# Converting 64-bit weights without a maximum and a mask, and a new order of the first query loads, in an attention and gated-layer kernel

## The chip, the cores and the metric

One Trainium2 chip, one core of it. The metric is the time of one execution on the device in microseconds (us); three runs of the kernel before give a median of 1798.62 us (1796.67 to 1802.75).

TensorE (PE in the rows) multiplies matrices, with its weight loads (PEld) beside it; VectorE is DVE, ScalarE is ACT, GpSimd is POOL, and SP is the engine that issues most transfers. TensorE writes to PSUM banks, the others read them from there; everything else lies in SBUF tiles.

## What is computed

Attention on keys and values pooled by 8, then a gated layer, then a layer with a rational activation, all in float32 accuracy:

```python
k_p = k.reshape(B, H, Sp, 8, D).mean(axis=3)      # B = H = 8, S = 576, D = 64
v_p = v.reshape(B, H, Sp, 8, D).mean(axis=3)
attn = softmax(q @ k_p.T / sqrt(D));  x = attn @ v_p        # 4608 tokens, 512 columns
g = x @ w_gate                                    # 512 x 1536
x = (g * sigmoid(g) * (x @ w_val)) @ w_out        # 1536 x 512
h = x @ w_in                                      # 512 x 2048
out = (P(h) / (Q(h) + 1e-6)) @ w_out2             # 2048 x 512
```

All weights come as 64-bit floating-point numbers, two 32-bit words each, and are converted on the chip.

## The kernel before

**Blocks.** The 4608 tokens are worked in 9 blocks of 512. Blocks 0 to 2 go one by one through the gated layer (`PLAIN = 3`, stages j = 0, 1, 2), the other six in pairs with a Strassen-like scheme whose sums of weights are made in stages 1 and 2 and streamed from DRAM. The last layer runs over all 9 blocks at the end.

**One step.** Each stage loops over f = 0 to 11, one 128-column part of the 1536. A step has 12 matmuls for the gate (`gp`), 12 for the value (`vp`) and 12 for the output (`acc`, of the step before). Each product is three: high by high, low by high, high by low part (`mm3`, line 256), so a weight is needed in two tiles, `w[:, 0]` (the high part, written by ScalarE, line 165) and `w[:, 1]` (the low part, a subtraction on VectorE, line 149). The first four matmuls of a product use the high parts alone; the next four need the low part of the weight. In stage 0 the step also converts the three weights of a later step (`first.step(6)` at three places of the step). VectorE has besides the gate's product `hh` (line 803) and the low part `ht` (line 808).

**Conversion of a weight** (`conversion`, from line 102). A raw tile holds the two words of each number. ScalarE takes the absolute value of the high word, read as float32 (L110), and scales the low word (L111). VectorE takes a maximum (L120), shifts left by 3 and masks (L121), and joins the sign (L114, `select`). GpSimd adds the low word (L117). The result goes to ScalarE for the high part and to VectorE for the low part. The tiles are called `tg`, `tv`, `to` and `rawg`, `rawv`, `rawo` for gate, value and output weights of the gated layer (36 conversions, 128 x 512, class `Weights`), and `rawi`, `rawo` for the last layer (64 conversions of 128 x 256, class `Halves`, in the later stages). In `Weights.step` the ScalarE part of one weight, the VectorE and GpSimd part of the one begun before, the rounding of the one before that and the last subtraction of a fourth stand one behind another.

**Attention.** A unit is up to 128 tokens of one batch entry. For block 0 there are four (0, 128, 256, 384), worked before the gated layer starts: scores (line 368, 32 products for two units), maximum and difference or scaled maximum (lines 376 to 385), exponential on ScalarE (389, 394), sum and reciprocal (401 to 403), normalisation on GpSimd (404), copies (412), transposes on TensorE (429, 433), their evacuation (436, 437, 441), and the products with the values (457, 460). The values are summed on VectorE (305) and masked on GpSimd (318 to 334). For block 1 the units 0 to 4 run inside stage 0, from f = 5 on, at fixed places of the step: scores behind one step, the maximum, the exponential and the sum in the next, the transposes (line 429) ahead of the value product of the one after.

**Order.** There is no scheduler: each engine's instructions run in the order in which the code writes them, and each queue issues its loads in order. A tile's buffer comes free when its last reader is done; a load into it waits for that in SP's queue.

Of the kernel before, what the change touches and what calls it, by code (L numbers as in the profile page):

```python
# [10 lines left out]
F32 = mybir.dt.float32  # L11
F32R = mybir.dt.float32r
U32 = mybir.dt.uint32
AF = mybir.ActivationFunctionType
ALU = mybir.AluOpType
# [48 lines left out]
def attention_gated_rational(  # L64
# [4 lines left out]
    nc = tc.nc  # L69
# [11 lines left out]
    def f32(ap):  # L81
        return ap.bitcast(F32)
# [14 lines left out]

    LEAST = float(np.uint32(0x38000000).view(np.float32))  # L100

    def conversion(key, raw, n, spare, t=None):

        hi_word, lo_word = raw[:, :, 1], raw[:, :, 0]
        if t is None:
            t = ldp.tile([P, 512], F32, tag="ld", name=f"t{key}")[:, :n]
        tu = t.bitcast(U32)

        def words():
            nc.scalar.activation(t, hi_word.bitcast(F32), AF.Abs)  # L110
            nc.scalar.activation(lo_word, lo_word, AF.Copy, scale=2.0 ** -29)  # L111

        def select():
            nc.vector.scalar_tensor_tensor(  # L114
                hi_word, hi_word, 0xC0000000, tu, op0=ALU.bitwise_and, op1=ALU.bitwise_or
            )
            nc.gpsimd.tensor_tensor(tu if spare else hi_word, hi_word, lo_word, op=ALU.add)  # L117

        bits = [
            lambda: nc.vector.tensor_scalar(t, t, LEAST, None, op0=ALU.max),  # L120
            lambda: nc.vector.tensor_scalar(  # L121
                tu, tu, 3, 0x3FFFFFFF, op0=ALU.logical_shift_left, op1=ALU.bitwise_and
            ),
            select,
        ]
        return words, bits, t if spare else f32(hi_word)

    class Weights:
# [14 lines left out]
        def step(self, ahead, eng=None):  # L143
            begun = None
            middle, rounded, last = self.stages
            if last:
                key, spare, _, t = last
                w = self.done[key]
                (eng or nc.vector).tensor_tensor(w[:, 1, :], t, f32(w[:, 0, :]), op=ALU.subtract)  # L149
                live["w"] -= not spare  # L150
            if self.raws:
                key, raw, spare = self.raws.pop(0)
                words, bits, t = conversion(key, raw, 512, spare)
                words()
                begun = key, spare, bits, t
            if middle:
                for fn in middle[2]:
                    fn()
                live["w"] -= middle[1]
            if rounded:  # L160
                live["w"] += 1
                assert live["w"] <= WSLOTS
                key, t = rounded[0], rounded[3]
                w = self.done[key] = wslot(f"w{key}")
                nc.scalar.activation(w[:, 0, :], t, AF.Copy)
            self.stages = [begun, middle, rounded]
            while self.next < len(self.items) and len(self.raws) < ahead:
                if live["w"] + (self.next < self.spare or any(x and not x[1] for x in self.stages)) >= WSLOTS:
                    break
                self.load()  # L170
# [5 lines left out]
    class Halves:  # L176
# [26 lines left out]
        def begin(self, n=1, more=1):  # L203
            self.store()
            for _ in range(more):
                self.load()
            self.now = []
            for key, h, tile_, raw in [self.raw.pop(0) for _ in range(min(n, len(self.raw)))]:
                t = f32(tile_[:, 512:768])
                words, bits, _ = conversion(f"{key}_{h}", raw, 256, True, t)  # L210
                words()
                self.now.append((key, h, tile_, t, bits))
# [57 lines left out]
    def at_load(src, name, early, n=512, eng=None, parts=P):  # L270
        t = wslot(name, (P, 512), F32) if early else ldp.tile([P, 512], F32, tag="ld", name=name)
        (eng or nc.sync).dma_start(t[:parts, :n], src)
        return t
# [201 lines left out]
    def qload(u, early=False, eng=None):  # L475
        b, s, n, o = u
        off = NPAIR * (b * S + s)
        return at_load(q[:, off : off + NPAIR * n], f"q{b}_{s}", early, NPAIR * n, eng)
# [50 lines left out]
    flat0 = [u for g in g0 for u in g]  # L529
    qts = {flat0[0]: qload(flat0[0], True, nc.scalar)}  # L530
    qts[flat0[1]] = qload(flat0[1], True)
    nc.scalar.dma_start(ident, ident_in)
    nc.scalar.dma_start(vmask, vmask_in)
    nc.scalar.activation(vr[:, :, 0, :], ident[:, :D].unsqueeze(1).to_broadcast([P, NPAIR, D]), AF.Copy, scale=0.0)
    vruns = [jb() for jb in jobs[5:]]
    for u in flat0[2:]:
        qts[u] = qload(u, True)
    nc.scalar.dma_start(cab[:, 0:4], ca)
    nc.scalar.dma_start(cab[:, 4:6], cb)

# [12 lines left out]
        r()  # L553
    x = [keep.tile([P, 2, BLK], F32R, tag=f"x{kk}", name=f"x0_{kk}") for kk in range(KT)]
    soft = [scores(u, qts[u], True, heads=n < 2) for n, u in enumerate(flat0)]
    for n in range(2):
        soft[n][0]()
        soft[n][1]()
    for r in vruns:
        r()  # L560
    build_vs(0)
# [7 lines left out]
        evacs[n] = transposes(flat0[n], ptTs[n], 0, 1 + n % 2)  # L569

    last = len(flat0)
    soft[0][2]()
    soft[0][3]()
    soft[2][0]()
    soft[2][1]()
    first.step(6)
    soft[1][2]()
    soft[1][3]()
# [437 lines left out]
    def hidden_part(p, key, k):  # L1016
        while order_h and len(ahead) < 3:
            nxt = order_h[0]
            if nxt[0] != p and nxt[2] == 0 and k < NK - 1:
                break  # L1020
            ahead.append(hidden_sum(*order_h.pop(0)))
        t = ring_tile(f"h{p}{key}_{k}")
        split(t[:, 0, :], t[:, 1, :], ahead.pop(0))
        return t
# [3 lines left out]
    for p, (j1, j2) in enumerate(PAIRS):  # L1028
# [36 lines left out]
        for i, (ow, key) in enumerate(zip(O_ORDER, TOKENS)):  # L1065
# [5 lines left out]
            for k in range(NK):  # L1071
                t = hidden_part(p, key, k)
# [29 lines left out]
    with tc.tile_pool(name="p2", bufs=1, reuse_waits="tile") as p2:  # L1102
# [31 lines left out]
        for n, (j, f) in enumerate(its):  # L1134
# [11 lines left out]
            t = p2.tile([P, BLK], F32, tag="t", name=f"t{n}")  # L1146
# [93 lines left out]
```

## Time and profile before

| | us |
|---|---|
| median of three runs | 1798.62 (1796.67 to 1802.75) |
| the profiled execution | 1798.48 |
| its span, first to last instruction | 1796.7 |
| TensorE busy | 1743.1 (97%) |
| VectorE busy | 1404.0 (78%) |
| ScalarE busy | 1135.4 (63%) |
| GpSimd busy | 345.4 (19%) |

The shares are means over stages with different limits. Of the page's 40 slices of 44.9 us, TensorE is busy 6, 8, 9 and 8 tenths in the first four, and 9 in all others but the last. The mean granted clock of TensorE is 0.996. So the page sends a reader to the first 180 us, and to the rows of that stretch.

### The profile page before, as it was taken

To read this page: it belongs to the slowest core of one execution; us is meant where nothing else is said; L and a number is where in the kernel's file an instruction comes from. 1 tells how busy PE (TensorE), PEld (TensorE's weight loads), DVE (VectorE), ACT (ScalarE), POOL (GpSimd) and SP (SyncE) were. 2 spreads that over 40 slices of the span, in tenths; PEclk is the share of its full clock that TensorE was granted. 3 is DMA by queue.
4 is the path that set the end of the run, shared out by engine and by line. 5 is a ranking of instruction groups with operands and counts; after the bars stand their busy time and mean duration, and the time that the engine had idled before them with its cause. 6 is when DMAs were issued, how large, how long until landed. Compare 5 with 4: busy or idle time off the path is not lost.

```text
span 1796.7 us, 23824 instructions
## 1 busy us (share of the span) xinstructions
PE 1743.1 (97%) x8212; PEld 1423.5 (79%) x8212; DVE 1404.0 (78%) x2333; ACT 1135.4 (63%) x1994; POOL 345.4 (19%) x492
## 2 busy tenths in 40 slices
PE   6898999999999999999999999999999999999998
PEld 5677877787887887887888788888888888888887
DVE  7997665548777676546777898989898989898987
ACT  5676455546665766435455676777677777767775
POOL 3344555542454344210000000000000000000000
PEclk9999999999999999999999999999999999999999
DMA  7631756559999898999826601010101010101000
GB/s 256 215 109 59 226 184 238 198 178 330 336 371 353 278 367 297 329 365 372 317 109 234 246 1 47 1 47 1 47 1 47 1 47 1 47 1 47 1 24 24
DMA packets 157464, 285.27 MB, mean 159 GB/s; under 512 B 12320, under 2 KB 78496, under 8 KB 156320
## 3 DMA queue, kind: packets, MB, share of 16 engines
q1 hardware_dynamic: 156624, 283.43, 44.8%
q8 instruction: 65, 1.06, 0.2%
q10 hardware_dynamic: 720, 0.33, 0.1%
q14 instruction: 55, 0.45, 0.1%
HBM read 194.58 MB, written 89.13 MB: 158 GB/s over the span
## 4 chain that ended last, share of the span: by engine, by line
PE 81%; DVE 5%; ACT 3%; issue 2%; POOL 1%; DMA 1%; POOLq 0%; DVEq 0%; ACTq 0%; SPq 0%
PE acco L256 22%; PE h L256 21%; PE ca L256 9%; PE ya L1083 5%; PE cc L256 5%; PE acc L256 3%; PE vp L256 3%; PE yc L1083 3%; PE gp L256 2%; PE cb L256 2%; PE pv L457 1%; PE yb L1083 1%; PE sc L368 1%; PE t L429 1%; DMA sw<-wd 0%
## 5 line engine op out<-in xcount | busy, mean ns | idle before, releaser
L256 PE MATMUL acco<-wo,gt 128*128 128x512 f32 x1728 | 417.3, 390 | 2.8 <-ACT gt L1170 2.4
L256 PE MATMUL h<-z,wi 128*128 128x512 f32 x1728 | 414.7, 389 | 0.0
L256 PEld LDWEIGHTS acco<-wo,gt 128*128 128x128 f32 x1728 | 325.3, 188 | 71.8 <-ACT gt L1170 3.2
L256 PEld LDWEIGHTS h<-z,wi 128*128 128x128 f32 x1728 | 324.4, 188 | 67.4
L1149 ACT ACTIVATE sq<-h 128x512 f32<-128x512 f32 x144 | 86.1, 598 | 197.3 <-PE h L256 197.3
L1156 DVE SCALAR_TENSOR_TENSOR w<-sq,neg,w 128x512 f32<-128x512 f32 x144 | 108.0, 750 | 48.2 <-ACT w L1150 48.2
L256 PE MATMUL vp<-x,wv 128*128 128x512 f32 x432 | 109.5, 401 | 6.2 <-DVE wv L149 6.2
L1166 DVE SCALAR_TENSOR_TENSOR g<-t,neg,e 128x512 f32<-128x512 f32 x144 | 108.3, 752 | 5.1
L1153 ACT ACTIVATE t<-h,neg 128x512 f32<-128x512 f32 x144 | 112.0, 778 | 0.0
L1162 DVE SCALAR_TENSOR_TENSOR t<-t,neg,h 128x512 f32<-128x512 f32 x144 | 107.7, 748 | 5.1
L256 PE MATMUL gp<-x,wg 128*128 128x512 f32 x432 | 108.0, 397 | 3.1 <-DVE wg L149 3.0
L1163 DVE SCALAR_TENSOR_TENSOR e<-w,ln 128x512 f32<-128x512 f32 x144 | 98.6, 685 | 13.5 <-ACT ln L1160 13.4
L1160 ACT ACTIVATE ln<-ln,lnb 128x512 f32<-128x512 f32 x144 | 104.3, 724 | 4.7
L256 PE MATMUL acc<-ht,wo 128*128 128x512 f32 x432 | 104.7, 391 | 0.0
L1170 ACT ACTIVATE gt<-g 128x512 fp32r<-128x512 f32 x144 | 90.8, 631 | 21.8 <-DVE g L1166 21.8
L1164 DVE SCALAR_TENSOR_TENSOR e<-e,ln 128x512 f32<-128x512 f32 x144 | 99.7, 692 | 5.0
L1150 ACT ACTIVATE w<-h,cab 128x512 f32<-128x512 f32 x144 | 98.3, 683 | 3.6 <-DVE e L1163 3.6
L256 PEld LDWEIGHTS vp<-x,wv 128*128 128x128 f32 x432 | 80.5, 191 | 25.3 <-DVE wv L149 8.7
L1171 DVE TENSOR_TENSOR gt<-g,gt 128x512 fp32r<-128x512 f32 x144 | 98.9, 687 | 1.9 <-ACT gt L1170 0.8
L1161 DVE TENSOR_TENSOR t<-t,h 128x512 f32<-128x512 f32 x144 | 98.2, 682 | 0.0
L256 PEld LDWEIGHTS gp<-x,wg 128*128 128x128 f32 x432 | 79.2, 188 | 22.8 <-DVE wg L149 5.1
L256 PEld LDWEIGHTS acc<-ht,wo 128*128 128x128 f32 x432 | 80.2, 188 | 16.7
(247 smaller groups left out, 3161.2 us busy)
## 6 DMA issues: line engine op xcount, KB each, us to landing
sw<-sd SPq DMA_DIRECT2D x72, 512.0 KB, 7.7
sw<-wd SPq DMA_DIRECT2D x36, 512.0 KB, 6.2
h<-hq SPq DMA_DIRECT2D x36, 512.0 KB, 7.8
sd<-sp SPq DMA_DIRECT2D x24, 512.0 KB, 4.3
sw<-vd SPq DMA_DIRECT2D x36, 256.0 KB, 7.8
hl<-h SPq DMA_DIRECT2D x18, 512.0 KB, 6.7
hr<-h SPq DMA_DIRECT2D x18, 512.0 KB, 9.7
out<-ob SPq DMA_DIRECT2D x36, 256.0 KB, 2.2
```

The lines of the kernel that those rows point to most:

```text
L256: nc.tensor.matmul(acc, st[:, lw, cols], mv[:, rw, mcols], start=first and i == 0, stop=last and i == n - 1, skip_group_check=seeded,)
L1083: nc.tensor.matmul(banks[q], w[:, lw, cols], t[:, rw, :], start=opened and k == 0 and m == 0, stop=k == NK - 1 and m == 2, skip_group_chec ...
L1150: nc.scalar.activation(w0, hps, AF.Abs, scale=cab[:, 4:5])
L1153: nc.scalar.activation(t, hps, AF.Identity, scale=neg[:, 3:4], bias=neg[:, 2:3])
L1156: nc.vector.scalar_tensor_tensor(w0, sq, neg[:, 5:6], w0, op0=ALU.mult, op1=ALU.add)
L1160: nc.scalar.activation(ln, ln, AF.Exp, scale=-1.0, bias=lnb)
L1161: nc.vector.tensor_tensor(t, t, hps, op=ALU.mult)
L1162: nc.vector.scalar_tensor_tensor(t, t, neg[:, 1:2], hps, op0=ALU.add, op1=ALU.mult)
L1163: nc.vector.scalar_tensor_tensor(e, w0, C1, ln, op0=ALU.add, op1=ALU.mult)
L1164: nc.vector.scalar_tensor_tensor(e, e, 2.0, ln, op0=ALU.subtract, op1=ALU.mult)
L1166: nc.vector.scalar_tensor_tensor(g, t, neg[:, 0:1], e, op0=ALU.add, op1=ALU.mult)
L1171: lambda gt=gt, g=g: nc.vector.tensor_tensor(gt[:, 1, :], g, f32(gt[:, 0, :]), op=ALU.subtract),
```

## The change

In `conversion` the factor 2^-112 is put into ScalarE's absolute value, the maximum with `LEAST` goes, and the shift loses its mask; `select` masks one bit of the high word instead of two. In the first loads, the queries of units 2 and 3 are asked for ahead of the values, and unit 2's maximum, difference and exponential, and unit 0's sum and normalisation, are written ahead of the values' sums.

```diff
-    LEAST = float(np.uint32(0x38000000).view(np.float32))
+    REBIAS = 2.0 ** -112
...
-            nc.scalar.activation(t, hi_word.bitcast(F32), AF.Abs)
+            nc.scalar.activation(t, hi_word.bitcast(F32), AF.Abs, scale=REBIAS)
...
-                hi_word, hi_word, 0xC0000000, tu, op0=ALU.bitwise_and, op1=ALU.bitwise_or
+                hi_word, hi_word, 0x80000000, tu, op0=ALU.bitwise_and, op1=ALU.bitwise_or
...
-            lambda: nc.vector.tensor_scalar(t, t, LEAST, None, op0=ALU.max),
-            lambda: nc.vector.tensor_scalar(
-                tu, tu, 3, 0x3FFFFFFF, op0=ALU.logical_shift_left, op1=ALU.bitwise_and
-            ),
+            lambda: nc.vector.tensor_scalar(tu, tu, 3, None, op0=ALU.logical_shift_left),
...
     qts[flat0[1]] = qload(flat0[1], True)
+    qts[flat0[2]] = qload(flat0[2], True, nc.scalar)
+    qts[flat0[3]] = qload(flat0[3], True)
     nc.scalar.dma_start(ident, ident_in)
...
-    for u in flat0[2:]:
-        qts[u] = qload(u, True)
...
-    for n in range(2):
+    for n in range(3):
         soft[n][0]()
         soft[n][1]()
+    soft[0][2]()
+    soft[0][3]()
     for r in vruns:
         r()
     build_vs(0)
...
-    soft[0][2]()
-    soft[0][3]()
-    soft[2][0]()
-    soft[2][1]()
     first.step(6)
```

Where this moves instructions, the order on the engine shows it. First VectorE in stage 0, within the step f = 1. L120 is the maximum, L121 the shift, L114 the join, L149 (L146 in the changed code) a low part, L803 (L798) the gate's product. Before:

```order
L120 TENSOR_SCALAR tg_633<-tg_633 128x512
L121 TENSOR_SCALAR tg_633<-tg_633 128x512
L114 SCALAR_TENSOR_TENSOR rawg_255<-rawg_255,tg_633 128x512
L149 TENSOR_TENSOR wo_659<-rawo_145,wo_659 128x512
L120 TENSOR_SCALAR tv_652<-tv_652 128x512
L121 TENSOR_SCALAR tv_652<-tv_652 128x512
L114 SCALAR_TENSOR_TENSOR rawv_290<-rawv_290,tv_652 128x512
L803 TENSOR_TENSOR hh_1_676<-hh_1_676,vp_1_690 128x512
L149 TENSOR_TENSOR wg_686<-rawg_255,wg_686 128x512
L120 TENSOR_SCALAR to_679<-to_679 128x512
L121 TENSOR_SCALAR to_679<-to_679 128x512
L114 SCALAR_TENSOR_TENSOR rawo_365<-rawo_365,to_679 128x512
```

After, from the same place on; L120 is now the shift:

```order
L120 TENSOR_SCALAR tg_628<-tg_628 128x512
L114 SCALAR_TENSOR_TENSOR rawg_255<-rawg_255,tg_628 128x512
L146 TENSOR_TENSOR wo_652<-rawo_145,wo_652 128x512
L120 TENSOR_SCALAR tv_646<-tv_646 128x512
L114 SCALAR_TENSOR_TENSOR rawv_289<-rawv_289,tv_646 128x512
L798 TENSOR_TENSOR hh_1_669<-hh_1_669,vp_1_682 128x512
L146 TENSOR_TENSOR wg_678<-rawg_255,wg_678 128x512
L120 TENSOR_SCALAR to_672<-to_672 128x512
L114 SCALAR_TENSOR_TENSOR rawo_363<-rawo_363,to_672 128x512
```

Three instructions of twelve are gone; the others stand in the same order, as they do in all of stage 0.

Second VectorE at the start, behind the maxima of units 0 and 1. `vp` are the value sums, `sm_0` the sum of unit 0, `mx_256` and `p_256` the maximum and difference of unit 2. Before, from the last two of six value sums on:

```order
L305 TENSOR_REDUCE vp_118<-v_4_125 96x64
L305 TENSOR_REDUCE vp_118<-v_5_127 96x64
L402 TENSOR_SCALAR sm_0_158<-sm_0_158 128x8
L403 RECIPROCAL sm_0_158<-sm_0_158 128x8
L376 TENSOR_REDUCE mx_256_183<-sc_256_0_185 128x4
L379 TENSOR_TENSOR p_256_182<-sc_256_0_185,mx_256_183 128x4x72
L376 TENSOR_REDUCE mx_256_183<-sc_256_1_186 128x4
L379 TENSOR_TENSOR p_256_182<-sc_256_1_186,mx_256_183 128x4x72
L402 TENSOR_SCALAR sm_128_171<-sm_128_171 128x8
L403 RECIPROCAL sm_128_171<-sm_128_171 128x8
```

After, with the first four of the six value sums at the end:

```order
L373 TENSOR_REDUCE mx_256_183<-sc_256_0_185 128x4
L376 TENSOR_TENSOR p_256_182<-sc_256_0_185,mx_256_183 128x4x72
L373 TENSOR_REDUCE mx_256_183<-sc_256_1_186 128x4
L376 TENSOR_TENSOR p_256_182<-sc_256_1_186,mx_256_183 128x4x72
L399 TENSOR_SCALAR sm_0_158<-sm_0_158 128x8
L400 RECIPROCAL sm_0_158<-sm_0_158 128x8
L302 TENSOR_REDUCE vp_122<-v_0_120 128x64
L302 TENSOR_REDUCE vp_122<-v_1_123 128x64
L302 TENSOR_REDUCE vp_122<-v_2_125 128x64
L302 TENSOR_REDUCE vp_122<-v_3_127 128x64
```

Unit 2's four instructions and unit 0's two moved ahead of the six value sums. On GpSimd unit 0's normalisation and copies moved ahead of the three instructions that mask the values in the same way.

Third SP's queue of loads, from the last keys on. Before:

```order
L272 DMA k_2048_107<-in_k 128x256
L272 DMA q_128_111<-in_q 128x512
L272 DMA v_0_116<-in_v 128x512
L272 DMA v_1_119<-in_v 128x512
L272 DMA v_2_121<-in_v 128x512
L272 DMA v_3_123<-in_v 128x512
L272 DMA v_4_125<-in_vrest 96x512
L272 DMA v_5_127<-in_vrest 96x512
L272 DMA q_256_129<-in_q 128x512
L272 DMA q_384_131<-in_q 128x512
```

After:

```order
L269 DMA k_2048_107<-in_k 128x256
L269 DMA q_128_111<-in_q 128x512
L269 DMA q_384_115<-in_q 128x512
L269 DMA v_0_120<-in_v 128x512
L269 DMA v_1_123<-in_v 128x512
L269 DMA v_2_125<-in_v 128x512
L269 DMA v_3_127<-in_v 128x512
L269 DMA v_4_129<-in_vrest 96x512
L269 DMA v_5_131<-in_vrest 96x512
```

The query of unit 3 moved ahead of the six value loads, and that of unit 2 left this queue: on ScalarE's queue it is now the second load, behind the query of unit 0 and ahead of `ident`.

## Rows read from the trace of the kernel before

**Rows 1.** Busy time by stage: length, each engine (instructions), granted clock, DMA share, GB/s

```profile
0.00:37.00 37.00, 20.43 (x137) 18.45 (x137) 25.70 (x63) 20.14 (x70) 12.76 (x22) 1.00 0.82 300
37.00:160.00 123.00, 108.53 (x526) 83.26 (x525) 119.58 (x209) 91.24 (x150) 50.26 (x48) 0.99 0.37 127
160.00:430.00 270.00, 262.11 (x1357) 210.69 (x1357) 162.92 (x304) 143.59 (x244) 133.17 (x219) 1.00 0.62 206
430.00:1797.00 1367.00, 1352.04 (x6196) 1111.15 (x6195) 1095.76 (x1759) 880.42 (x1533) 149.20 (x204) 1.00 0.42 148
```

**Rows 2.** Waits of TensorE, 37 to 172 us: total, times, longest

```profile
PE t L429 <- POOL p L404: 6.3, 4, 2.4
PE vp L256 <- DVE wv L149: 6.2, 6, 2.0
```

**Rows 3.** Timeline of TensorE, 98 to 177 us: waits ahead of products, two starts

```profile
100.60 2.12 PE L256 MATMUL vp<-x,wv 128*128 128x512 f32 x8 [1.97 <-DVE wv L149]
...
111.42 0.46 PE L429 MATMUL t<-ident,p 64*128 64x64 f32 x4 [1.99 <-POOL p L404]
...
137.30 0.66 PE L429 MATMUL t<-ident,p 128*128 128x128 f32 x4 [1.68 <-POOL p L404]
...
150.53 0.72 PE L433 MATMUL t<-ident,pr 128*96 128x128 f32 x2 [0.48 <-POOL pr L412]
...
161.81 0.46 PE L429 MATMUL t<-ident,p 64*128 64x64 f32 x4 [2.35 <-POOL p L404]
...
172.66 2.88 PE L256 MATMUL gp<-x,wg 128*128 128x512 f32 x12
175.38 1.98 PE L256 MATMUL vp<-x,wv 128*128 128x512 f32 x8
```

**Rows 4.** Timeline, step f = 1: start, us, engine, line, out<-in, count, idle before

```profile
48.14 0.68 DVE L149 TENSOR_TENSOR wv<-rawv,wv 128x512 fp32r<-128x512 f32 x1
...
48.74 0.42 DVE L120 TENSOR_SCALAR tg<-tg 128x512 f32<-128x512 f32 x1
...
49.19 0.43 DVE L121 TENSOR_SCALAR tg<-tg 128x512 uint32<-128x512 uint32 x1
...
50.48 1.37 POOL L117 TENSOR_TENSOR rawg<-rawg 128x512 uint32<-128x512 uint32 x1 [2.55 <-DVE rawg L114]
...
50.87 1.27 DVE L120 TENSOR_SCALAR tv<-tv 128x512 f32<-128x512 f32 x1
...
58.28 0.69 DVE L149 TENSOR_TENSOR wv<-rawv,wv 128x512 fp32r<-128x512 f32 x1
```

**Rows 5.** Timeline of VectorE and TensorE in the first 23 us

```profile
10.54 0.82 DVE L376 TENSOR_REDUCE mx<-sc 128x4 f32<-128x288 f32 x2 [0.68 <-PE sc L368]
...
15.22 3.69 PE L368 MATMUL sc<-kr,q 64*128 64x72 f32 x32 [4.71 <-DMA q<-in_q]
...
17.24 0.46 DVE L376 TENSOR_REDUCE mx<-sc 128x4 f32<-128x288 f32 x1 [1.48 <-PE sc L368]
...
22.09 0.38 DVE L120 TENSOR_SCALAR tg<-tg 128x512 f32<-128x512 f32 x1
...
22.50 1.25 DVE L121 TENSOR_SCALAR tg<-tg 128x512 uint32<-128x512 uint32 x1
```

**Rows 6.** Busy time as in Rows 1, 114 to 116 us

```profile
114.00:116.00 2.00, 2.00 (x6) 1.60 (x5) 1.97 (x3) 1.99 (x5) 1.04 (x1) 0.50 0.00 0
```

**Rows 7.** Line 120, one tile: duration ns min/median/max, first and last start, forms

```profile
L120 DVE TENSOR_SCALAR rawi<-rawi x32: 280/286/1378, 174.0 to 807.0; 128x256 f32<-128x256 f32 x32
```

**Rows 8.** Timeline of ScalarE: loads of the gate's activation table

```profile
124.95 1.28 ACT L793 ACT_TABLE_LOAD   x1
...
136.43 1.28 ACT L793 ACT_TABLE_LOAD   x1
...
148.52 1.28 ACT L793 ACT_TABLE_LOAD   x1
```

**Rows 9.** Busy time as in Rows 1, the paired blocks

```profile
430.00:835.00 405.00, 396.81 (x1995) 321.74 (x1995) 262.21 (x510) 234.53 (x447) 149.20 (x204) 0.99 0.96 341
```

## The prediction

> **What bounds the kernel now.** I first read the busy time by stage [rows 1]. From 160 us on TensorE is busy 262.11 of 270 us and then 1352.04 of 1367: nothing there can be gained by helping another engine. The loss sits ahead of it. In the first 37 us attention of block 0 runs and TensorE is busy for 20.43. From 37 to 160, block 0 of the gated layer, TensorE is busy 108.53 of 123 and VectorE 119.58 of 123, ScalarE 91.24, GpSimd 50.26. So in that stage the reader should see VectorE as the engine that is never idle.
>
> Then the waits of TensorE there [rows 2]: it waits 6.2 us for the low parts that VectorE writes of `wv`, and 6.3 us for the normalised scores of GpSimd, which wait for sums that stand in VectorE's queue. Both go back to VectorE. The work of one step f without attention is 36 matmuls; 12 of them start 2.72 us apart from the next 12 [rows 3], so 8.16 us, while VectorE's round, from one low part of `wv` to the next, is 58.28 - 48.14 = 10.14 us [rows 4]. I call that a round: round f runs from the value product of f to that of f + 1.
>
> **The conversions.** The change takes one VectorE instruction, the maximum (L120), out of each conversion of weights; the mask went along as a second operation of the shift (L121), and its leaving costs or saves nothing that a row separates: the maximum with one operation takes 0.42 us and the shift with two 0.43 [rows 4]. The factor 2^-112 rides on a ScalarE instruction that is there already. There are 36 conversions of 512 columns, 3 of which are through VectorE before 37 us, and 64 of 256 columns later.
>
> What one maximum is worth: with a free port, the shift starts 49.19 - 48.74 = 0.45 us after it [rows 4]. With a GpSimd instruction in flight it is longer: the maximum of `tv` at 50.87 takes 1.27 us and ends at 52.14, 0.29 us after GpSimd's `rawg` instruction (50.48 + 1.37) [rows 4]. Counting durations, a round would shed 0.42 + 1.27 + 0.42 = 2.1 us. I don't take that: GpSimd's instruction is released by VectorE's own previous conversion, so it stands at the same place in the round after the change, and the shift, an instruction of the same kind, walks into it. A row shows a shift so held: 1.25 us at 22.50 [rows 5]. Each conversion then sheds 0.45, held or not, a round with three sheds 1.35, and all 33 after 37 us shed 14.9 us of VectorE time.
>
> The Trainium skill ("SBUF — State Buffer", section "Who interferes with whom") says that GpSimd shares a port pair with VectorE instructions in two-port modes, tensor_scalar among them, as an exclusive lock, where the later one blocks fully. By that rule too the hold passes to the shift; without it the sum would be 2.1 us a round, some 20 us in all. The holds at 50.87 and 22.50 agree with it.
>
> How much of 14.9 us reaches TensorE goes round by round. **Rounds 0 to 4** (no attention in them): 10.14 - 1.35 = 8.79 us against TensorE's 8.16, so VectorE still sets the pace and all comes through: 5 x 1.35 = 6.75 us. **Rounds 5 to 10** also carry block 1's attention, on all engines. Here the gap of TensorE that ends a round says how much it can take: 1.97, 1.99, 1.68 and 2.35 us for rounds 5, 6, 8 and 10 [rows 3], each more than 1.35, so 4 x 1.35 = 5.4. Round 9, which has a value product of 256 columns, ends with a gap of 0.48 [rows 3]: TensorE is nearly full, 0.5. Round 7 ends without a gap of note, because its 12 matmuls after 112 us ran at a granted clock of 0.50 (1.2 of 2.4 GHz) in 114 to 116 [rows 6], right after the gap of 1.99. With shorter gaps ahead it may run at full clock or not; between nothing and 1.35 I take 0.7. Sum: 6.75 + 5.4 + 0.5 + 0.7 = 13.35 us; bounds 9 (half of the attention rounds fails) and 14.9.
>
> The 64 later conversions shed 0.28 us each [rows 7], 18 us of VectorE, which costs and gives nothing: VectorE is busy 162.92 of 270 us there and TensorE full [rows 1]. If TensorE's small gaps there follow VectorE, 1.5 us more could come; as the phases of engines shift, 1 us could be lost. I take 0.
>
> **The first loads.** Queries of unit 2 now go out on ScalarE's queue, second, ahead of `ident` and `vmask`; those of unit 3 on SP's queue ahead of the six value loads. Before, TensorE's third and fourth score products waited 4.71 us for that query until 15.22, and VectorE idled 1.48 us until 17.24 for them [rows 5]. That idle time goes. In its place VectorE, which now has unit 2's maximum and difference ahead of the value sums, stands and waits for unit 2's scores; behind it stand the six value sums, and behind those GpSimd's masked values. Before, the value sums filled this time. 32 score products take 3.69 us [rows 5], so one unit's 16 some 1.85; Unit 1's scores end shortly before VectorE reads them at 10.54 [rows 5], so unit 2's would be there at about 12.4; VectorE, done with unit 1's two maxima (0.82 us) and one small instruction at about 11.5, idles 0.9 to 1.1. Net 0.4 us gained. The bound below nothing: 256 KB more among the keys, at the 300 GB/s of this stretch [rows 1], is 0.9 us of delay to the first scores, so 0.5 us lost. GpSimd normalises unit 0 earlier but unit 1 no earlier, since the masked values now stand ahead of it. ScalarE issues one load more ahead of `ident`; its first use of that tile must only end before unit 0's exponentials, which wait for VectorE's maxima anyway.
>
> The Trainium skill ("DMA: Bandwidth & Descriptors", "Issuing engines are not separate DMA queues") says that loads of ScalarE and SP interleave on the same 16 engines. By that rule the query's bytes do delay the keys; without it nothing would be lost there. No row here tells the two apart.
>
> In this stretch VectorE also sheds the maximum of `tg` (0.41 us, 22.09 to 22.50) [rows 5], which stands ahead of unit 3's sum and unit 0's low part, and one of two later ones on the path, 0.4. The shift at 22.50 may be held less (0.82) or a later small instruction more; zero. Sum: 0.4 + 0.4 + 0.4 = 1.2 us earlier, between 0.5 later and 3.0 earlier.
>
> **Sum.** 13.35 + 1.2 = 14.55 us. The profiled execution took 1798.48 us (span 1796.7), 0.14 from the median of 1798.62. 1798.5 - 14.5 = 1784 us; its own range, from the bounds, is 1781 to 1788.
>
> **The rivals.** (a) ScalarE takes over in the attention rounds. Two activation tables are loaded in each; from the load for the gate to the next such load are 148.52 - 136.43 = 12.09 us [rows 8], and I want 12.09 - 1.35 = 10.74. One round earlier it was 136.43 - 124.95 = 11.48 [rows 8], so at least 0.6 us of the 12.09 was waiting, and over the stage ScalarE has 31.8 of 123 us free [rows 1]; if its waits don't close, rounds 6 to 9 give a third: 13.35 falls to 9.5, so 1788 us. (b) More: the half-clock stretch goes away, the start wins 3 us, and TensorE's later gaps close: 18 to 19 us, 1780. (c) The gain is given back: from 430 to 835 us the DMA engines are busy 0.96 of the time [rows 9]; were weight streaming the bound there and not released by TensorE's progress, it would end where it does now and the time stay at some 1797. Against it: TensorE is busy 396.81 of 405 us there [rows 9]. (d) Slower: the holds by GpSimd multiply. A held shift costs 1.25 - 0.43 = 0.82 us more [rows 4, 5]; had each of 33 shifts one hold more than its conversion has now, that is 27 us against the 14.9 shed, and the kernel ends at some 1810. From 18 new holds on it is slower. Against it: two of three in a round are free now, for GpSimd is 50.26 of 123 us busy [rows 1], and the order that makes it so doesn't move.
>
> **How the numbers follow.** Forecast 0.60, (a) 0.15, (b) 0.15, (c) 0.05, (d) 0.05. The likeliest is 1784. The range runs from (b), 1780, to a little beyond (a), 1790. A measurement of this kernel tells 0.3%, 5.4 us, from no change: faster is the forecast, (a) and (b) plus what of (c) gives back only half, 0.92; same 0.04; slower 0.04.
>
> **What would show it.** In the profile after, VectorE's rounds without attention should be 8.7 to 8.9 us long, with the shift of `tv` at some 1.27; TensorE's gaps at `wv` some 0.2 to 0.5; the first product of the gated layer at 35 to 36.5 us; block 1's first product (172.66 now [rows 3]) at about 158; and everything behind that at the same distances. Wrong would be: rounds that stay above 9.5 us, shifts of `tg` and `to` held as well, or a difference that grows or shrinks by over 2 us between 160 us and the end.

## The result and the profile after

The changed kernel takes 1780.43 us (median of four runs, 1778.96 to 1780.78), the kernel before 1799.45 us (four runs, 1796.67 to 1802.75): a ratio of 0.9892, with a 95% interval of 0.9874 to 0.9910, 19.0 us less. Its profiled execution took 1780.39 us with a span of 1778.6, against 1798.48 and 1796.7: 18.1 us less in the two profiles. The forecast was 1784 with a range of 1780 to 1790: the direction and the range hold, and the time lies at the range's lower end, 3.6 us under the forecast. It is nearer to rival (b), 1780, and just below the forecast's own bounds, 1781 to 1788.

First the busy time by stage of the changed kernel, as in [rows 1] (length; TensorE, its weight loads, VectorE, ScalarE, GpSimd; granted clock, DMA share, GB/s); the cuts lie at about the same places of the work, which come earlier now.

```profile
0.00:35.70 35.70, 21.07 (x136) 19.28 (x137) 23.79 (x60) 20.25 (x70) 12.74 (x22) 1.00 0.85 311
35.70:145.70 110.00, 105.42 (x527) 82.59 (x525) 104.00 (x178) 90.37 (x150) 49.80 (x49) 1.00 0.43 142
145.70:415.10 269.40, 261.90 (x1357) 210.69 (x1357) 156.87 (x290) 142.96 (x244) 133.15 (x219) 1.00 0.62 206
```

In block 0's stage VectorE was busy 119.58 of 123 us, and TensorE 108.53; now they are busy 104.00 and 105.42 of 110. Neither is idle for long: they bound the stage together. The waits of TensorE, 35 to 157 us (total, times, longest), answer to [rows 2]:

```profile
PE t L426 <- POOL p L401: 3.6, 4, 1.5
PE vp L253 <- DVE wv L146: 1.9, 5, 0.6
```

They were 6.3 and 6.2. In the timeline of TensorE the waits of [rows 3] and the first product of block 1 are these (start, duration, engine, line, operation, count, wait ahead):

```profile
91.13 2.11 PE L253 MATMUL vp<-x,wv 128*128 128x512 f32 x8 [0.55 <-DVE wv L146]
...
100.56 0.46 PE L426 MATMUL t<-ident,p 64*128 64x64 f32 x4 [0.61 <-POOL p L401]
...
124.33 0.66 PE L426 MATMUL t<-ident,p 128*128 128x128 f32 x4 [0.88 <-POOL p L401]
...
146.97 0.46 PE L426 MATMUL t<-ident,p 64*128 64x64 f32 x4 [1.48 <-POOL p L401]
...
157.79 2.43 PE L253 MATMUL gp<-x,wg 128*128 128x512 f32 x10
```

The step f = 1 on VectorE and GpSimd, where [rows 4] had a round of 10.14 us:

```profile
45.62 0.68 DVE L146 TENSOR_TENSOR wv<-rawv,wv 128x512 fp32r<-128x512 f32 x1
...
46.22 0.42 DVE L120 TENSOR_SCALAR tg<-tg 128x512 uint32<-128x512 uint32 x1
...
47.50 1.36 POOL L117 TENSOR_TENSOR rawg<-rawg 128x512 uint32<-128x512 uint32 x1 [2.09 <-DVE rawg L114]
...
47.89 1.26 DVE L120 TENSOR_SCALAR tv<-tv 128x512 uint32<-128x512 uint32 x1
...
50.01 1.04 POOL L117 TENSOR_TENSOR rawv<-rawv 128x512 uint32<-128x512 uint32 x1 [1.15 <-DVE rawv L114]
...
50.39 1.21 DVE L146 TENSOR_TENSOR wg<-rawg,wg 128x512 fp32r<-128x512 f32 x1
...
54.37 0.68 DVE L146 TENSOR_TENSOR wv<-rawv,wv 128x512 fp32r<-128x512 f32 x1
```

The round is 54.37 - 45.62 = 8.75 us. The maximum of `tv`, which was held to 1.27 us, is gone, and the shift behind it is held to 1.26 in its place: both start 0.39 us after GpSimd's `rawg` instruction. The low part of `wg` is held too, 1.21 instead of 0.68, as GpSimd's `rawv` instruction is in flight. That hold is not new; in the same round of the kernel before it stands as well:

```profile
53.84 1.21 DVE L149 TENSOR_TENSOR wg<-rawg,wg 128x512 fp32r<-128x512 f32 x1
```

At the start, where [rows 5] had VectorE idle 1.48 us ahead of unit 2's maximum, and a held shift:

```profile
9.25 0.82 DVE L373 TENSOR_REDUCE mx<-sc 128x4 f32<-128x288 f32 x2 [0.89 <-PE sc L365]
...
12.94 0.46 DVE L373 TENSOR_REDUCE mx<-sc 128x4 f32<-128x288 f32 x1 [0.95 <-ACT p L391]
...
21.92 0.42 DVE L120 TENSOR_SCALAR tg<-tg 128x512 uint32<-128x512 uint32 x1
...
22.38 0.69 DVE L114 SCALAR_TENSOR_TENSOR rawg<-rawg,tg 128x512 uint32<-128x512 uint32 x1
...
22.43 1.64 POOL L401 TENSOR_TENSOR p<-p,sm 128x576 f32<-128x576 f32 x1
```

Now one table for all profiles that follow. Its marks are starts of products in TensorE's timeline: the first gate product; block 1's first; the first pair's first product on `x0t` (into `cc`); the second pair's first on `x1t` into `ca`; the third's first on `x2t` (into `cc`); the first on `h0b`. Each column is the time from mark to mark; "lost" is the sum of length x (1 - granted clock) over 2 us rows, in block 0's stage, at the change to the second pair, and around the products on `x2b` shortly ahead of `h0b`.

| profile | to first gate product | block 0 | to x0t | to x1t | to x2t | to h0b | lost |
|---|---|---|---|---|---|---|---|
| before | 36.99 | 135.67 | 245.5 | 147.2 | 147.0 | 118.3 | 1.70, 3.42, 0 |
| before, again | 37.01 | 137.92 | 245.5 | 147.2 | 147.3 | 118.3 | 5.12, 3.42, 0 |
| after | 35.73 | 122.06 | 245.5 | 146.9 | 144.9 | 117.4 | 0, 1.72, 0 |
| after, again | 35.63 | 122.08 | 245.5 | 146.8 | 144.9 | 117.0 | 0, 1.72, 0 |
| conversion alone | 36.92 | 123.62 | 245.6 | 146.8 | 144.9 | 117.2 | 1.70, 1.70, 0 |
| loads alone | 37.20 | 135.61 | 245.5 | 147.3 | 147.2 | 121.2 | 1.70, 3.42, 1.70 |
| gated weights alone | 36.81 | 122.10 | 245.4 | 147.2 | 147.4 | 118.2 | 0, 3.42, 0 |
| last weights alone | 37.01 | 138.35 | 245.5 | 146.8 | 144.9 | 118.2 | 3.42, 1.70, 0 |
| one maximum at the change | 35.13 | 123.62 | 245.5 | 146.9 | 145.2 | 120.1 | 1.72, 1.70, 1.72 |
| three maxima at the change | 35.14 | 122.00 | 245.4 | 146.8 | 147.4 | 117.3 | 0, 3.40, 0 |
| one maximum at the start | 36.71 | 122.06 | 245.5 | 146.8 | 146.4 | 116.6 | 0, 3.40, 0 |
| mask kept | 35.17 | 122.05 | 245.4 | 146.8 | 144.8 | 117.1 | 0, 1.72, 0 |
| no GpSimd addition | 35.35 | 117.98 | 245.5 | 146.8 | 144.8 | 121.0 | 0, 1.72, 1.70 |
| no GpSimd addition, again | 36.08 | 119.55 | 245.5 | 146.8 | 144.9 | 117.1 | 1.70, 1.70, 0 |

From `h0b` to the end all take 964.4 to 966.6 us. Of the 18.1 us between the two spans 1.26 were gained ahead of the first gate product, 13.61 in block 0's stage, 0.4 in the first pair, 2.1 at the change to the second pair, 0.9 behind it, and none between blocks 1 and 2 and from `h0b` on (0.1 was lost there).

### The profile page after: what moved, and what is told of

It reads as the page before. It is cut to its first block, busy times and chain, and to the rows that moved or that the text cites. A ratio compares the mean times of both kernels' runs of the same rounds, so it can differ in the third digit from the quotient of the medians.

```text
span 1778.6 us, 23734 instructions
## 1 busy us (share of the span) xinstructions
PE 1738.8 (98%) x8212; PEld 1422.2 (80%) x8212; DVE 1363.9 (77%) x2233; ACT 1134.3 (64%) x1994; POOL 341.7 (19%) x492
## 3 DMA queue, kind: packets, MB, share of 16 engines
q8 instruction: 65, 1.06, 0.2%
## 4 chain that ended last, share of the span: by engine, by line
PE 83%; DVE 7%; ACT 3%; issue 3%; POOL 2%; DMA 1%; SPq 0%; POOLq 0%; DVEq 0%; ACTq 0%
PE acco L253 22%; PE h L253 22%; PE ca L253 9%; PE ya L1078 5%; PE cc L253 5%; PE vp L253 3%; PE acc L253 3%; PE gp L253 3%; PE yc L1078 3%; PE cb L253 2%; PE pv L454 2%; PE sc L365 1%; PE yb L1078 1%; PE t L426 1%; DVE vp L302 1%
```

## The experiments

My theory: VectorE paces block 0, each of its maxima is worth 0.45 us there and the order of the loads some 0.4. What was not foreseen was some 3.3 us gained behind 400 us. Rival A put that down to the maxima missing there, rival B to the moment at which the stage is reached, or to the granted clock.

**Each part alone.** The conversion alone (the kernel before with the diff's lines of `conversion`):

> The new conversion with the old order of first loads. Theory 1 (VectorE paces block 0, each maximum is worth 0.45 us, the load order some 0.4 us): block 0's stage from its first gate product to block 1's first is 13.6 us shorter than before, as in the changed kernel; the start 0.8 us shorter; later stages as in the changed kernel; in all 17 to 18 us faster than before. Rival (the load order carries the start's gain): the start is unchanged or later and the whole 16.5 us faster or less.

Measured: 1781.10 us, against 1798.63 of the kernel before (ratio 0.9903, 0.9890 to 0.9917), 17.5 less. Block 0's stage is 12.05 us shorter and not 13.6, as 1.70 were lost at half clock there, behind a wait of 1.48. The loads alone (the kernel after with the old lines of `conversion`):

> The new order of first loads with the old conversion. Theory 1: the first gate product some 0.4 us earlier, stage of block 0 unchanged within 0.5 us, in all 0 to 1 us faster. Rival (load order carries the start's gain): 1.2 us earlier. Rival (keys are delayed and the idle time only moves): 0.5 us later.

Measured: 1800.44 us, ratio 1.0008 (1.0000 to 1.0017). In the table its first gate product comes 0.2 us later than before, and the conversion's alone 0.07 earlier, yet with both it comes 1.26 earlier: the start's gain is not the sum of the parts. The keys' arrival blurs these numbers. The first maximum on scores starts at 8.83 us in the profile of before, at 9.12 with the conversion alone, although its loads are the old ones, and at 9.25 with the loads alone and in the changed kernel. From there to the first gate product are 28.16 us before, 27.80 with the conversion alone, 27.95 with the loads alone, and 26.48 with both: 0.4, 0.2 and 1.7 less.

**Half of the conversions each.** One flag picks the new lines:

```
+        new = n == 512     # or n == 256
+            nc.scalar.activation(t, hi_word.bitcast(F32), AF.Abs, scale=REBIAS if new else 1.0)
...
+        if new:
+            bits = [lambda: nc.vector.tensor_scalar(tu, tu, 3, None, op0=ALU.logical_shift_left), select]
```

Only the 36 gated-layer weights (n == 512), then only the 64 weights of the last layer (n == 256):

> The new conversion for the 36 weights of the gated layer alone; the 64 conversions of the last layer and the loads as before. Theory A (the 3.2 us gained after 500 us come from the maxima missing from VectorE at the change of pairs): 14.4 us faster than before, and the stretch from the second pair's first product to the third pair's as long as before, 147 us. Theory B (they come from the phase or from the clock of the one execution): some 17.5 us faster, or that stretch at 145 us although its conversions are the old ones.

> The new conversion for the 64 of the last layer alone; the 36 and the loads as before. Theory A: 3 us faster than before, with block 0 unchanged and the stretch between the pairs at 145 us. Theory B: no difference, 147 us.

Measured: 1784.85 us (ratio 0.9927, 0.9913 to 0.9940), 13.8 less, and 1797.38 (0.9988, 0.9979 to 0.9997). With the gated weights alone block 0's stage is that of the changed kernel, 122.10, and the change of pairs that of before, 147.4. With the last weights alone the change of pairs has the new length, 144.9: rival A is right that the later maxima count. The median shows 1.3 us against the 3 expected, and the profile (span 1797.4) none, because 2.7 are lost in block 0's stage, where nothing was changed; its busy time there (columns as above):

```profile
160.00:162.00 2.00, 0.17 (x2) 0.17 (x3) 0.75 (x2) 1.97 (x3) 1.65 (x2) 0.88 0.00 0
162.00:164.00 2.00, 2.00 (x9) 1.66 (x10) 0.90 (x2) 1.08 (x3) 1.92 (x5) 0.50 0.00 0
164.00:166.00 2.00, 2.00 (x6) 1.52 (x6) 0.23 (x1) 0.00 (x0) 1.84 (x4) 0.50 0.00 0
166.00:168.00 2.00, 2.00 (x7) 1.52 (x6) 0.00 (x0) 0.00 (x0) 0.00 (x0) 0.50 0.00 0
168.00:170.00 2.00, 2.00 (x14) 2.00 (x13) 0.69 (x1) 0.49 (x1) 0.00 (x0) 0.91 0.00 0
```

TensorE stood still for the wait that was 2.35 us in [rows 3], 2.38 here, and then ran for 6 us at half clock (1.2 of 2.4 GHz), with VectorE idle beside it for most of the time: 2.7 of the 3.4 us lost show in the stage. In the profile of before the half-clock rows stood at 112 to 118 (the middle one in [rows 6]), and the next wait of TensorE was only 0.33 us; here it is 1.90 at the same product. So there the slow stretch was paid out of a wait for VectorE that came anyway.

**The change of pairs.** One maximum put back into the changed kernel, in the conversion of the weight `o2_7_0`, ahead of the low parts of `x1t`:

```
+        if key in ('o2_7_0',):
+            bits.insert(0, lambda: nc.vector.tensor_scalar(t, t, 0.0, None, op0=ALU.max))
```

> The changed kernel with one maximum (against zero, which changes no value) put back, in the single conversion of 256 columns that VectorE works at the change from the first pair of blocks to the second. In the profiles that stretch, from the second pair's first product on x1t to its product on x2t, took 147.0 us before and 144.9 after, though only one maximum of 0.29 us has left it ahead of the low parts of x1t. Theory 1 (the single instruction lengthens TensorE's wait for those low parts, and the stretch at a granted clock of 0.50 behind it becomes longer): the stretch goes back to 147, all else stays, 1782.5 us, 2 us slower than the changed kernel. Theory 2 (the many maxima ahead of it, or the moment at which the stage is reached, decide): the stretch stays at 144.9 to 145.3 and the time at 1780.4 to 1780.8.

Measured: 1781.97 us (ratio 0.9908, 0.9894 to 0.9921), and 145.2 at the change. The time alone would have spoken for theory 1, but the table shows the extra in two half-clock stretches elsewhere. The one instruction lengthens TensorE's wait by 0.33 us and no more. Three maxima put back (`i2_7_0`, `i2_7_1`, `o2_7_0`):

> The changed kernel with three maxima (against zero, which changes no value) put back at the change of pairs: two ahead of the low parts of x1b, at 546.8 and 547.5 us, and the one ahead of the low parts of x1t, at 556.5. The one alone brought TensorE's wait for x1t back from 0.71 to 1.04 us and the stretch from 144.9 to 145.2. In the three profiles with all later maxima TensorE has one wait more, of 0.49 to 0.53 us at x1b's products, and the stretch takes 147.0 to 147.4. Theory 1 (the two maxima ahead of x1b make that wait, and the longer stretch at half clock follows the waits): the wait of 0.5 is back, and the stretch is 147. Theory 2 (the waits come from those instructions, but the length of the half-clock stretch isn't theirs): the wait of 0.5 is back, and the stretch is 145.7.

Measured: 1781.94 us (ratio 0.9904, 0.9887 to 0.9920), and 147.4 at the change, all of the 2.1 us and a little more, for 0.85 us of VectorE. TensorE's waits there, in the changed kernel and with three maxima (the row of `x1b` names no engine that ended its wait):

```profile
557.95 1.49 PE L253 MATMUL ca<-x1t,sw 128*128 128x512 f32 x4 [0.26 <-ACT x1t L93]
560.15 0.50 PE L253 MATMUL ca<-x1t,sw 128*128 128x512 f32 x1 [0.71 <-DVE x1t L94]
561.70 0.50 PE L253 MATMUL ca<-x1t,sw 128*128 128x512 f32 x1 [1.06 <-DVE x1t L94]
```

```profile
554.13 1.65 PE L255 MATMUL cc<-x1b,sw 128*128 128x512 f32 x6 [0.52 <-issue]
...
557.80 1.48 PE L255 MATMUL ca<-x1t,sw 128*128 128x512 f32 x4 [0.26 <-ACT x1t L93]
...
560.32 0.50 PE L255 MATMUL ca<-x1t,sw 128*128 128x512 f32 x1 [1.04 <-DVE x1t L94]
...
561.88 0.72 PE L255 MATMUL ca<-x1t,sw 128*128 128x512 f32 x1 [1.05 <-DVE x1t L94]
```

The waits grow from 2.03 to 2.87 us, and behind them come the rows at half clock, in the changed kernel and with three maxima:

```profile
562.20:564.20 2.00, 2.00 (x21) 1.73 (x21) 1.96 (x4) 0.00 (x0) 0.47 (x1) 0.88 0.76 293
564.20:566.20 2.00, 2.00 (x6) 1.61 (x5) 1.58 (x4) 0.49 (x2) 0.00 (x0) 0.50 1.01 240
566.20:568.20 2.00, 2.00 (x11) 1.57 (x11) 0.29 (x1) 1.39 (x5) 0.00 (x0) 0.76 0.97 334
```

```profile
561.40:563.40 2.00, 1.52 (x9) 1.09 (x11) 1.19 (x3) 0.00 (x0) 1.44 (x3) 0.65 0.83 329
563.40:565.40 2.00, 2.00 (x14) 1.74 (x13) 1.95 (x4) 0.00 (x0) 0.00 (x0) 0.50 0.73 208
565.40:567.40 2.00, 2.00 (x6) 1.55 (x5) 0.92 (x3) 0.00 (x0) 0.00 (x0) 0.50 0.93 233
567.40:569.40 2.00, 2.00 (x7) 1.50 (x7) 0.00 (x0) 1.89 (x5) 0.00 (x0) 0.65 0.99 314
```

1.72 us lost against 3.40. Over all 14 profiles: the five with the three maxima lose 3.40 to 3.42 there, eight of the nine without all three lose 1.70 to 1.72. The ninth (one maximum at the start) has the short waits, loses 3.40 and takes 146.4. So the waits belong to the instructions, and the longer slow stretch follows them nearly always, but not by them alone.

**The same two kernels again.**

> The kernel before, as it is, for a second profile. Theory 1 (the time between marks belongs to the code): 135.7 us in block 0's stage, 147.0 at the change of pairs and 118.3 from there to the product on h0b, each within 0.3. Theory 2 (half-clock stretches and late transfers fall differently from execution to execution): block 0's stage anywhere from 135.6 to 138.4 (the latter was seen where the half-clock stretch lay behind the last wait), the other two 1 to 3 us off.

> The changed kernel, as it is, for a second profile and beside the others on one chip. Theory 1 (code): 122.1, 144.9 and 117.4 us between the same marks, each within 0.3. [...]

Measured: 1801.0 us for before (one execution), 1780.12 for after (ratio 0.9899, 0.9885 to 0.9914). At the change of pairs both repeat within 0.3, and behind it within 0.4. Block 0's stage of before took 2.25 us more: 5.12 us were lost at half clock in three stretches, one of them behind the stage's last wait. So one stage of one code differs by over 2 us between executions.

**The start.** One maximum put back, in the first gate weight's conversion (`g0`), in the same way:

> The changed kernel with one maximum (against zero, which changes no value) put back, in the first gate weight's conversion, at 21.9 us. Conversion alone moved the first product of the gated layer by 0.07 us, the order of the loads alone by 0.2 the other way, both together by 1.26 earlier. Theory 1 (a race of VectorE and GpSimd: in the changed kernel the shift and the join are through before GpSimd's normalisation holds VectorE, and with 0.45 us more they are not): the join takes 1.5 us instead of 0.69 and the first product of the gated layer comes at 37.0, 1.3 us later for one instruction of 0.42; 1781.7 us. Theory 2 (the parts just add up): it comes 0.45 us later, at 36.2, and the time is 1780.9.

Measured: 1781.18 us (ratio 0.9910, 0.9895 to 0.9924). The first gate product comes at 36.71, 1.0 to 1.6 us later than in the five profiles of kernels with the new loads and conversion and no maximum there (35.13 to 35.73). VectorE and GpSimd with that maximum (L124):

```profile
21.98 0.43 DVE L124 TENSOR_SCALAR tg<-tg 128x512 f32<-128x512 f32 x1
...
22.44 0.43 DVE L120 TENSOR_SCALAR tg<-tg 128x512 uint32<-128x512 uint32 x1
22.49 1.38 POOL L403 TENSOR_TENSOR p<-p,sm 128x576 f32<-128x576 f32 x1
22.90 1.52 DVE L114 SCALAR_TENSOR_TENSOR rawg<-rawg,tg 128x512 uint32<-128x512 uint32 x1
```

The join is held to 1.52 us, until GpSimd's normalisation is through. In the changed kernel (its rows are in the section on the result) the join begins 0.05 us ahead of the normalisation, takes 0.69, and GpSimd waits in its place: 1.64 us. One instruction of 0.43 costs 1.29 us on VectorE (0.46 for itself, 0.83 for the hold), since it loses the race. The conversion alone and the loads alone each lose it as well: their joins take 1.52.

**The mask.**

```
+            lambda: nc.vector.tensor_scalar(
+                tu, tu, 3, 0x7FFFFFFF, op0=ALU.logical_shift_left, op1=ALU.bitwise_and
+            ),
```

> The changed kernel with a mask kept as the second operation of the shift (a mask that leaves the value as it is). Theory 1 (an instruction costs by its columns and its place, a second operation is free): shifts of 512 columns stay at 0.42 to 0.43 us where nothing holds them, and the time stays within 1 us of 1780.4. Theory 2 (the second operation costs): each of 100 shifts is longer, and the rounds without attention leave 8.75 us.

Measured: 1778.99 us (1777.26 to 1780.29), the same shifts (mean 422, 956 and 492 ns for `tg`, `tv`, `to`; 423, 955 and 492 without the mask) and the same block 0 stage. The second operation of this shift is free.

**GpSimd's addition taken out.** In the 36 conversions of 512 columns VectorE joins the low word itself, and ScalarE rounds it down (`bias=-0.4999` with its scale):

```
+                lambda: nc.vector.scalar_tensor_tensor(
+                    tu, tu, 3, lo_word, op0=ALU.logical_shift_left, op1=ALU.bitwise_or
+                ),
```

> The changed kernel without GpSimd's addition of the low word in the 36 conversions of 512 columns: VectorE joins the low word in the shift's instruction, which has then two operands of 512 columns (0.69 us like the join, instead of 0.42), and ScalarE rounds the low word down. A round of the changed kernel has three unheld instructions at 0.42, one of them held to 1.27, and one low part held to 1.21 instead of 0.68. Theory 1 (these holds are GpSimd's addition): both vanish, 0.85 + 0.53 less, against 3 x 0.27 more: VectorE's round falls by 0.57 from 8.75 to some 8.2, TensorE's 8.16 is then the pace, the stage of block 0 sheds some 3 to 5 us, 1775 to 1778 us in all. Theory 2 (the long ones are not holds by that addition): they stay, the rounds grow by 0.8, and the time is some 1788 us.

> The kernel without GpSimd's addition in the conversions of 512 columns once more, beside the changed kernel on one chip. Its block 0 stage took 118.0 us against 122.1, but a wait of 3.0 us for a streamed weight and a half-clock stretch behind it made the part after the change of pairs 121.0 instead of 117.4. Theory 1 (that wait varies with the execution): 118.0 again in block 0's stage, the median 2 to 4 us under the changed kernel's. Theory 2 (the earlier arrival causes the wait each time): 121 again there and a median within 1 us of the changed kernel's.

Measured: 1777.44 us (ratio 0.9876, 0.9859 to 0.9893), then, beside the changed kernel's 1780.12, 1778.30 (1775.21 to 1780.05; ratio 0.9883, 0.9868 to 0.9898). VectorE in step f = 1:

```profile
45.49 0.68 DVE L159 TENSOR_TENSOR wv<-rawv,wv 128x512 fp32r<-128x512 f32 x1
...
48.02 0.69 DVE L131 SCALAR_TENSOR_TENSOR tv<-tv,rawv 128x512 uint32<-128x512 uint32 x1
...
49.94 0.69 DVE L159 TENSOR_TENSOR wg<-rawg,wg 128x512 fp32r<-128x512 f32 x1
...
53.67 0.68 DVE L159 TENSOR_TENSOR wv<-rawv,wv 128x512 fp32r<-128x512 f32 x1
```

Both holds are gone: they were GpSimd's addition. The round shrinks from 8.75 to 53.67 - 45.49 = 8.18 us, TensorE's own pace, and block 0's stage takes 118.0, or 119.55 with 1.70 lost at half clock. It is faster than the kernel before. That it is faster than the changed kernel, by some 1.8 us on one chip, is likely from the stage's 2.5 to 4.1 us but not settled by the times: the intervals overlap. The wait of 3.0 us at the products on `x2b` was 0.8 the second time, so it isn't what this edit causes each time. It is 0.3 to 3.0 us over all profiles, and a half-clock stretch follows in the three where it is over 2. Some rows put it down to the streamed weight `sw` and others to a conversion, but in all 14 it ends 0.13 to 0.14 us after a load of `sw` lands. In the changed kernel that load is issued at 781.22 and takes 8.2 us (product, issue, and the issue's size and time to landing):

```profile
789.54 1.63 PE L253 MATMUL ca<-x2b,sw 128*128 128x512 f32 x6 [1.00 <-DVE rawi L114]
781.22 0.33 SPq L739 DMA_DIRECT2D sw<-wd  x1
sw<-wd SPq DMA_DIRECT2D x1, 512.0 KB, 8.2
```

The load takes 8.2 us in eleven profiles and 8.65 to 9.20 in the three with the long wait. Why it does stays open.

## Where the prediction was right, and where not

**The conversions in block 0: right, and the closeness is luck.** 13.35 us were forecast and 13.61 came. Every step of it can be read: a round of 8.75 us where 8.79 was worked out, the hold passed on to the shift (1.26), the gaps at `wv` 0.26 to 0.55, with one round without, where 0.2 to 0.5 was said. By rounds, from value product to value product of the two profiles: rounds 0 to 4 shed 0.80, 1.24, 1.38, 1.38 and 1.48, 6.28 us against 6.75. Rounds 5 to 10 shed 0.51, 2.81, 1.28, 0.84, 1.00 and 0.87, 7.31 against 6.6. So the sum hides two small errors. And between the second profiles of both kernels the stage differs by 15.84 us, with the conversion alone by 12.05: half clock in one execution or the other moves it by 2. In rounds 8 and 10 I credited 1.35 and got 0.84 and 0.87, and TensorE still waits 0.88 and 1.48 us there: rival (a) in a small way, for VectorE now waits for ScalarE's high parts of `wg`, which it did not do before (waits of VectorE, 35 to 157 us):

```profile
DVE wg L146 <- ACT wg L162: 1.9, 2, 1.1
```

In round 9 I took its gap, 0.48, as all that it could give, and it gave 1.00. Rounds 5 and 6 together gave 3.32 against 2.7; the gap of 1.97 at 100.60, which I gave to round 5, stands behind the value product of 6 at 97.56 and so in round 6. The half-clock rows at 114 to 116, whose end I priced at 0.7 in round 7, are gone, and round 7 gave 1.28. The price of rival (a) does not follow from its terms: rounds 6 to 9 stand in the sum with 3.9, a third of it leaves 10.75 of the 13.35 and not 9.5, so 1786.5.

**Rival (d) fell, with one thing right in it.** The holds did not multiply in the stage. But at the start a hold can fall on the join as well, which the prediction did not consider. The Trainium skill ("SBUF — State Buffer", "Who interferes with whom") has this: a VectorE instruction with two inputs in SBUF contends with a GpSimd instruction that reads SBUF, and who comes first keeps the ports. I weighed only its sentence on tensor_scalar. The runs agree with the wider one: join 1.52 against 0.69, low part 1.21 against 0.68, and GpSimd's own normalisation 1.64 instead of 1.15 where it comes second.

**The start: the right number for wrong terms, by luck.** 1.2 us were forecast, as three terms of 0.4, and 1.26 came. They do not add up: counted from the first maximum the loads alone gain 0.2 and the conversion alone 0.4, both together 1.7, and the keys come 0.4 later. The step that failed is "the shift at 22.50 may be held less (0.82) or a later small instruction more; zero". This was the term that decided: 0.83 us of hold on VectorE, and what waits behind it, vanish when both edits together bring the join ahead of GpSimd's normalisation. The idle of 0.95 us ahead of unit 2's maximum has the length of the forecast, but its row names ScalarE's exponentials (`p` L391) and not unit 2's scores: `mx` has two buffers, unit 2's is unit 0's, and it comes free with unit 0's last exponential. The keys' delay shows too: the first maximum starts at 8.79 to 9.12 us in five profiles with the old order of loads and at 9.09 to 9.36 in nine with the new, 0.4 later by the medians. It lies inside the bound of 0.9. The delay agrees with the sentence of the Trainium skill that the prediction named ("DMA: Bandwidth & Descriptors", "Issuing engines are not separate DMA queues").

**The later 64 conversions: a term mis-sized.** I took 0, with 1.5 us at most; 3.3 came, and it is nearly all of the 3.6 us by which the forecast missed. By the prediction's own sign, a difference that grows by over 2 us between 160 us and the end, it was wrong here. The step was "VectorE is busy 162.92 of 270 us there and TensorE full": a mean over a stage, and over 160 to 430 us, while these conversions go on until 807 [rows 7] and the change of pairs lies in [rows 9]. At the change of pairs TensorE waits for VectorE's low parts of `x1b` and `x1t`, which stand behind three conversions, and the three maxima there lengthen TensorE's waits by 0.84 us. The other half is the clock: the slow stretch behind the waits loses 1.7 us less. Three maxima put back there return 2.5 us, which shows it for the waits; that the clock's part comes with them rests on five profiles of five against one of nine. Of the 0.9 us further on, 0.29 is a wait at the first products on `x2t` that is there with the later maxima and gone without. With the wait at the products on `x2b` and the 1.7 us of a half-clock stretch behind it taken off, the stretch to `h0b` is 117.1 to 117.2 us in the four profiles with the old later conversions and 116.2 to 116.4 in the ten with the new: 0.8 of the 0.9 is theirs. So is the 0.4 of the first pair, 147.2 to 147.3 in those four and 146.8 to 146.9 in the ten. So (b) held in part, and its 1780 is what was measured: the half-clock stretch of block 0 is gone and later gaps closed, but the start won 1.26 and not 3, and half of the later gain is clock, where I had not looked for it.

**Rival (c) fell:** everything from `h0b` on keeps its distances, and the paired blocks end earlier with the same DMA share, 0.96, as [rows 9] had it:

```profile
415.10:816.70 401.60, 394.99 (x1995) 320.80 (x1995) 245.76 (x459) 234.79 (x447) 146.04 (x204) 1.00 0.96 344
```

## What to carry to other kernels

Where an instruction of one engine can hold one of another, cost a removed instruction by the race that it wins or loses behind it, not by its duration: 0.43 us was worth 1.3, and two edits that were worth 0.4 and 0.2 alone were worth 1.7 together. A stage that is full on the mean still has places where another engine is last; look at each change of phase before writing a zero. And read a gain of 2 us against the stretches of granted clock in both profiles, stage by stage, before giving it to the edit.

## What was not expected of the hardware

- Up to the products on `h0b`, every stretch at half clock in the 14 profiles lost 1.7 us, or 3.4: no value between. Ahead of each, or into its start, TensorE had waited, for 1.48 to 3.02 us at once or, at the change of pairs, a few times for 0.26 to 1.06. The same wait is followed by one in one execution and not in another: the wait of 1.48 to 1.51 us that ends round 10 in two of eight profiles. And a wait of 3.8 us that ends at 22 us is followed by none in nine profiles.
- Whether such a stretch costs anything hangs on who is late next: 1.7 us lost at 112 to 118 us in the profile of before is paid by a shorter wait, 3.40 lost at 24 to 32 us with the last weights alone cost nothing (first gate product at 37.01), and 3.42 lost behind the last wait of block 0's stage cost 2.7.
- The mask as the second operation of VectorE's shift costs nothing (512 columns of uint32, 0.42 us with and without).
